# Transposes moved from TensorE to the DMA crossbar in a fused linear-attention and feed-forward kernel

## The chip, the cores and the metric

The kernel runs on one core of a Trainium2 chip. The metric is the device time of one execution in microseconds, median over several executions. An execution over 1.5% above the fastest of its kernel is called slow, and the others fast. A core has TensorE (PE, with its weight loads PEld), VectorE (DVE), ScalarE (ACT), GpSimd (POOL) and the sync engine (SP), and 16 DMA engines; the profile gives the packets of each DMA queue as a share of these 16 (it can sum to over 100%). Three queues issue DMAs here: sync's (q1), GpSimd's (q0) and, in one experiment, ScalarE's (q10). The granted clock is the share of its full speed that TensorE was given, as the trace records it.

## The reference, cut to what matters

```python
# q, k, v: (8 batches, 8 heads, 576 rows, 64), float32
phi(x)  = concat(relu(x) * cos_w, relu(x) * sin_w)      # 128 features per row
kv      = einsum('bhsf,bhsd->bhfd', phi(k), v);  z = sum of phi(k) over the rows
x       = (phi(q) @ kv) / (phi(q) @ z + 1e-6)           # -> (4608, 512)
out     = (((x @ w1) * (x @ w2)) @ w3) @ w_out          # -> (4608, 512)
```

The kernel transposes the left operand of two products, which has its rows on the partitions: the q features before `phi(q) @ kv`, and x before `x @ w1`. Each batch has five row chunks, four of 128 rows and one of 64.

## The kernel before: the parts that matter

`w3 @ w_out` is folded once. Then come the attention of batch 0 alone, step 0 of the feed-forward part (512 rows), the attention of batch 1 alone, and steps 1 to 8. Into step t, for t from 1 to 6, the attention of batch t + 1 is woven, and the loads of batch t + 3 are issued at its start (up to batch 7, so in steps 1 to 4).

```python
def load(b, eng):                       # k, v, q of one batch: 3 x (1 MB + 128 KB)
    ...
load(0, nc.gpsimd); ...w1, w2...; load(1, nc.gpsimd)     # cut; batches 2 to 7: nc.sync

def prep_k(b, c):                       # features of k; v gets a column of ones
    nc.vector.tensor_scalar(out=kp[...], in0=ks, ...)
    nc.scalar.activation(out=kp[...], in_=ks, func=ACTF.Relu, ...)
    nc.gpsimd.tensor_copy(out=va[:R, c, :, 0:D], in_=vs)

def q_tr(b, c):                         # transpose 8 heads of one chunk; cut: R, qp
    pst = ps_tr.tile([P, 8, 128], BF16, name="pst")
    for h in range(H):
        nc.tensor.transpose(pst[:, h, 0:R], qp[:R, c, h, :], identb[:R, :R])
    nc.vector.tensor_copy(out=att[b]["qpT"][:, :, ds(128 * c, R)], in_=pst[:, :, 0:R])

def num(b, c): ...                      # PE: numerator and denominator; DVE: den, xblk

def x_tr(b, c):                         # ... cut: which xT tile, which columns
    for kc in range(4):
        nc.tensor.transpose(pst[:, kc, 0:R], xf[:, ts(kc, 128)], identb[:R, :R])
    nc.scalar.copy(out=xT[t][:, :, ds(o, R)], in_=pst[:, 0:4, 0:R])

for t in range(NT):                     # cut: step 0, the bounds of t
    spread(prep_units(t + 2), 0, 22, slots); load(t + 3, nc.sync)
    spread(attention_units(t + 1), 0, 22, slots)   # 24 slots of a step
```

Of the kernel before, what the change touches and what calls it, by code (L numbers as in the profile page):

```python
# [11 lines left out]
BF16 = mybir.dt.bfloat16  # L12
# [4 lines left out]
P = 128  # L17
H, S, D = 8, 576, 64
F = 2 * D
NCH = 5  # L20
# [28 lines left out]
def kernel(  # L49
# [11 lines left out]
    nc = tc.nc  # L61
# [13 lines left out]
    ps_tr = ctx.enter_context(tc.tile_pool(name="ps_tr", bufs=2, space=bass.MemoryType.PSUM))  # L75
# [17 lines left out]
    identb = const.tile([P, P], BF16, name="identb")  # L93
# [11 lines left out]
    for i in range(2):  # L105
        va = const.tile([P, NCH, H, D + 1], BF16, name=f"va{i}")
# [4 lines left out]
    def load(b, eng):  # L111
        got = []
        for name, src in (("k", k), ("v", v), ("q", q)):
            t = ld.tile([P, H, 4, D], FP32, name=name + "s")
            eng.dma_start(out=t[:], in_=src[b, :, 0:512, :].rearrange("h (p j) d -> p h j d", j=4))
            t4 = ld.tile([64, H, D], FP32, name=name + "s4")
            eng.dma_start(out=t4[:], in_=src[b, :, 512:S, :].rearrange("h p d -> p h d"))
            got.append((t, t4))
        raw[b] = got
# [40 lines left out]
    def prep_k(b, c):  # L160

        R = ROWS[c]
        if c == 0:
            feat[b] = (
                phi.tile([P, NCH, H, F], BF16, name="kp"),
                phi.tile([P, NCH, H, F], BF16, name="qp"),
                va_bufs[b % 2],
            )
        kp, qp, va = feat[b]
        (k0, k4), (v0, v4), _ = raw[b]  # L170
        ks = k0[:, :, c, :] if c < 4 else k4[:]
        vs = v0[:, :, c, :] if c < 4 else v4[:]
        nc.vector.tensor_scalar(out=kp[:R, c, :, 0:D], in0=ks, scalar1=0.0,
                                scalar2=cosv[:R, c:c + 1], op0=ALU.max, op1=ALU.mult)
        nc.scalar.activation(out=kp[:R, c, :, D:F], in_=ks, func=ACTF.Relu,  # L175
                             scale=sinv[:R, c:c + 1], bias=0.0)
        nc.gpsimd.tensor_copy(out=va[:R, c, :, 0:D], in_=vs)  # L177

    def prep_q(b, c):

# [9 lines left out]
    att = {}  # L190

    def kv_chunk(b, c):
        R = ROWS[c]
        kp, qp, va = feat[b]
        if c == 0:
            att[b] = {
                "kv": ps_att.tile([P, 2, 512], FP32, name="pnum"),
                "qpT": phi.tile([P, H, S], BF16, name="qpT"),
                "x": {},
            }  # L200
        kvt = att[b]["kv"]
        for h in range(H):
            nc.tensor.matmul(kvt[:, h // 4, ds((h % 4) * 65, 65)], lhsT=kp[:R, c, h, :],  # L203
                             rhs=va[:R, c, h, :], start=(c == 0 and h % 4 == 0),
                             stop=(c == NCH - 1 and h % 4 == 3))
        if c == NCH - 1:
            kvs = sm.tile([P, H, D + 1], BF16, name="kvs")
            nc.scalar.copy(out=kvs[:, 0:4, :], in_=kvt[:, 0, 0:260])
            nc.vector.tensor_copy(out=kvs[:, 4:8, :], in_=kvt[:, 1, 0:260])
            att[b]["kvs"] = kvs  # L210

    def q_tr(b, c):
        R = ROWS[c]
        qp = feat[b][1]
        pst = ps_tr.tile([P, 8, 128], BF16, name="pst")
        for h in range(H):
            nc.tensor.transpose(pst[:, h, 0:R], qp[:R, c, h, :], identb[:R, :R])  # L217
        nc.vector.tensor_copy(out=att[b]["qpT"][:, :, ds(128 * c, R)], in_=pst[:, :, 0:R])  # L218

    def num(b, c):  # L220
        R = ROWS[c]
        qpT, kvs = att[b]["qpT"], att[b]["kvs"]
        nt = ps_att.tile([P, 2, 512], FP32, name="pnum")
        for h in range(H):
            nc.tensor.matmul(nt[:R, h // 4, ds((h % 4) * 65, 65)], lhsT=qpT[:, h, ds(128 * c, R)],  # L225
                             rhs=kvs[:, h, :], start=True, stop=True)
        n4 = nt[:R, :, 0:260].rearrange("p g (h e) -> p g h e", e=65)
        den = sm.tile([P, 2, 4], FP32, name="den")
        nc.vector.tensor_scalar_add(out=den[:R], in0=n4[:, :, :, 64], scalar1=1e-6)
        nc.vector.reciprocal(out=den[:R], in_=den[:R])  # L230
        xblk = sm.tile([P, 2, 4, D], BF16, name="xblk")
        nc.vector.tensor_tensor(out=xblk[:R], in0=n4[:, :, :, 0:D],  # L232
                                in1=den[:R].unsqueeze(3).to_broadcast([R, 2, 4, D]), op=ALU.mult)
        att[b]["x"][c] = xblk

    xT = {}

    def x_tr(b, c):
        R = ROWS[c]
        xblk = att[b]["x"].pop(c)  # L240
        xf = xblk[:R].rearrange("p g h d -> p (g h d)")
        if b % 2 == 0:
            slot = S * b + 128 * c
        else:
            slot = S * b + (0 if c == 4 else 64 + 128 * c)
        t, o = divmod(slot, 512)
        if t not in xT:
            xT[t] = xtp.tile([P, 4, 512], BF16, name="xT")
        pst = ps_tr.tile([P, 8, 128], BF16, name="pst")
        for kc in range(4):  # L250
            nc.tensor.transpose(pst[:, kc, 0:R], xf[:, ts(kc, 128)], identb[:R, :R])  # L251
        nc.scalar.copy(out=xT[t][:, :, ds(o, R)], in_=pst[:, 0:4, 0:R])  # L252

    def attention_units(b):

        order = [0, 1, 2, 3, 4] if b % 2 == 0 else [4, 0, 1, 2, 3]
        u = [(lambda c=c: kv_chunk(b, c)) for c in range(NCH)]
        u.insert(2, lambda: q_tr(b, order[0]))
        u.insert(5, lambda: q_tr(b, order[1]))
        for i in range(NCH + 1):  # L260
            if i < NCH:
                u.append(lambda c=order[i]: num(b, c))
            if i + 2 < NCH:
                u.append(lambda c=order[i + 2]: q_tr(b, c))
            if i >= 1:
                u.append(lambda c=order[i - 1]: x_tr(b, c))
        return u
# [42 lines left out]
    def prep_units(b):  # L310
        return ([(lambda c=c: prep_k(b, c)) for c in range(NCH)]
                + [(lambda c=c: prep_q(b, c)) for c in range(NCH)])
# [5 lines left out]
    for u in prep_units(0) + attention_units(0):  # L318
        u()

    def spread(units, first, last, slots):
        for i, u in enumerate(units):
            slots[min(last, first + int(i * (last + 1 - first) / len(units)))].append(u)

    for t in range(NT):
        slots = [[] for _ in range(24)]
        if t == 0:
            spread(prep_units(1), 15, 23, slots)
            slots[23] += prep_units(2)[0:4] + attention_units(1) + prep_units(2)[4:]
            load(2, nc.sync)  # L330
        else:
            if t + 2 < B:
                spread(prep_units(t + 2), 0, 22, slots)
                if t + 3 < B:
                    load(t + 3, nc.sync)
            if t + 1 < B:
                spread(attention_units(t + 1), 0, 22, slots)
        for g, _ in enumerate(ffn_groups(t)):
            for u in slots[g]:
                u()  # L340
        if t == 0:
            load(3, nc.sync)
# [30 lines left out]
```

## Time and profile before

| | before |
|---|---|
| median time (4 runs) | 306.85 us |
| span of the profiled run | 302.6 us |
| PE busy, share of the span | 89% |
| attention of batch 0 begins / step 0 / step 1 / step 2 begin | 43.5 / 57.7 / 93.5 / 120.9 us |
| a step with attention / without | 27.2 / 20.7 us |

The start of a step is the start of its first matmul with `w1b`. In the profile's lines "<-" inside a name pair reads "written from", and "idle before <- X" names what ended an engine's idle time. The lines that bound the kernel stand in the prediction.

### The profile page before, as it was taken

How to read it: one execution, taken by the hardware profiler on the slowest of the kernel's cores; microseconds unless marked ns; L12 is line 12 of the kernel's file. 1: busy time of each engine (PE TensorE's matmuls, PEld its weight loads, DVE VectorE, ACT ScalarE, POOL GpSimd, SP SyncE). 2: the span in 40 equal slices, each digit the busy share in tenths (PEclk: the TensorE clock that was granted, in tenths of full speed). 3: DMA queues.
4: the chain of work that ended last, by engine and by line, in shares of the span. 5: the costliest groups of instructions: out<-in, count | busy, mean ns of one | idle time of the engine just before them, and what ended most of it. 6: DMA issues, size and time to landing. Idle time of an engine off the chain costs nothing.

```text
span 302.6 us, 5330 instructions
## 1 busy us (share of the span) xinstructions
PE 268.1 (89%) x2112; PEld 145.0 (48%) x2112; DVE 160.6 (53%) x358; ACT 143.2 (47%) x249; POOL 45.8 (15%) x76
## 2 busy tenths in 40 slices
PE   1979027899877999999999999999999999999994
PEld 1444026444554554555555555555555555444441
DVE  7122607435677894488369637846872572330420
ACT  2033801335927756556656655575564225333322
POOL 8622650231004040012004000400000000000000
PEclk9999757599979999999999999999999999999999
DMA  7999999990499943791397269320013002103103
GB/s 99 194 277 276 212 257 289 261 230 9 143 287 269 268 112 96 211 267 54 131 289 178 68 192 264 88 109 32 0 44 97 2 0 105 37 0 118 23 15 124
DMA packets 41784, 43.33 MB, mean 143 GB/s; under 512 B 10848, under 2 KB 34912, under 8 KB 41760
## 3 DMA queue, kind: packets, MB, share of 16 engines
q1 hardware_dynamic: 33472, 30.68, 37.7%
q0 software_dynamic: 8288, 12.32, 19.4%
q8 instruction: 16, 0.26, 0.4%
q14 instruction: 8, 0.07, 0.1%
HBM read 38.80 MB, written 9.44 MB: 159 GB/s over the span
## 4 chain that ended last, share of the span: by engine, by line
PE 77%; DMA 11%; ACT 4%; DVE 3%; POOL 3%; issue 1%; POOLq 0%; ACTq 0%
PE ffnps L292 21%; PE ffnps L299 21%; PE ffnps L285 20%; DMA w2b<-in_moe_w_dram 5%; DMA ks<-in_k_dram 5%; PE pst L217 5%; PE pnum L225 4%; PE pnum L203 3%; PE pst L251 3%; DVE xblk L232 2%; ACT qp L187 1%; ACT kp L175 1%; POOL woutb L97 1%; POOL w3b L96 1%; DVE den L230 0%
## 5 line engine op out<-in xcount | busy, mean ns | idle before, releaser
L294 DVE TENSOR_TENSOR abT<-asb,ffnps 128x512 bf16<-128x512 bf16 x72 | 49.3, 685 | 71.8 <-PE ffnps L292 68.7
L288 ACT CAST asb<-ffnps 128x512 bf16<-128x512 f32 x72 | 42.1, 585 | 73.9 <-PE ffnps L285 67.6
L285 PE MATMUL ffnps<-xT,w1b 128*128 128x512 bf16 x288 | 74.7, 382 | 0.1
L292 PE MATMUL ffnps<-xT,w2b 128*128 128x512 bf16 x288 | 74.8, 382 | 0.0
L299 PE MATMUL ffnps<-w34b,abT 128*128 128x512 bf16 x288 | 69.6, 379 | 0.0
L177 POOL CAST va<-vs 128x512 bf16<-128x512 f32 (+1 forms) x40 | 24.3, 652 | 125.0 <-DMA vs<-in_v_dram 66.2
L285 PEld LDWEIGHTS <-w1b 128*128 128x128 bf16 x288 | 26.3, 98 | 25.9 <-issue 1.1
L299 PEld LDWEIGHTS <-abT 128*128 128x128 bf16 x288 | 26.2, 98 | 25.8
L292 PEld LDWEIGHTS <-w2b 128*128 128x128 bf16 x288 | 25.1, 98 | 24.3 <-issue 1.1
L252 ACT COPY xT<-pst 128x512 bf16<-128x512 bf16 (+1 forms) x40 | 21.8, 545 | 26.2 <-PE pst L251 25.2
L218 DVE COPY qpT<-pst 128x1024 bf16<-128x1024 bf16 (+1 forms) x40 | 25.2, 629 | 15.3 <-PE pst L217 15.3
L304 ACT COPY osb<-ffnps 128x512 f32<-128x512 f32 x36 | 21.1, 586 | 22.6 <-PE ffnps L299 16.1
L203 PE MATMUL pnum<-va,kp 128*128 128x65 bf16 (+1 forms) x320 | 17.2, 198 | 13.5 <-POOL va L177 13.5
L232 DVE TENSOR_TENSOR xblk<-pnum,den 128x512 bf16<-128x512 f32 (+1 forms) x40 | 27.6, 689 | 1.4
L187 ACT ACTIVATE qp<-qs,sinv 128x512 bf16<-128x512 f32 (+1 forms) x40 | 27.8, 720 | 0.2 <-DMA qs<-in_q_dram 0.2
L175 ACT ACTIVATE kp<-ks,sinv 128x512 bf16<-128x512 f32 (+1 forms) x40 | 27.8, 720 | 0.0
L203 PEld LDWEIGHTS <-kp 128*128 128x128 bf16 (+1 forms) x320 | 15.1, 101 | 22.8 <-issue 14.8
L217 PE MATMUL pst<-identb,qp 128*128 128x128 bf16 (+1 forms) x320 | 25.0, 225 | 0.9 <-ACT qp L187 0.8
L217 PEld LDWEIGHTS <-qp 128*128 128x128 bf16 (+1 forms) x320 | 20.7, 103 | 9.4 <-issue 1.3
L225 PE MATMUL pnum<-kvs,qpT 128*128 128x65 bf16 (+1 forms) x320 | 18.0, 200 | 5.4 <-DVE xblk L232 3.1
L225 PEld LDWEIGHTS <-qpT 128*128 128x128 bf16 (+1 forms) x320 | 15.4, 104 | 15.4 <-DVE xblk L232 4.9
L185 DVE TENSOR_SCALAR qp<-qs,cosv 128x512 bf16<-128x512 f32 (+1 forms) x40 | 21.0, 548 | 1.2 <-DMA qs<-in_q_dram 1.2
(46 smaller groups left out, 145.3 us busy)
## 6 DMA issues: line engine op xcount, KB each, us to landing
out_dram<-osb SPq DMA_DIRECT2D x32, 256.0 KB, 2.3
ks<-in_k_dram SPq DMA_DIRECT2D x6, 1024.0 KB, 8.0
vs<-in_v_dram SPq DMA_DIRECT2D x6, 1024.0 KB, 10.4
qs<-in_q_dram SPq DMA_DIRECT2D x6, 1024.0 KB, 10.8
ks<-in_k_dram POOLq DMA_DIRECT2D x2, 1024.0 KB, 17.6
vs<-in_v_dram POOLq DMA_DIRECT2D x2, 1024.0 KB, 21.2
qs<-in_q_dram POOLq DMA_DIRECT2D x2, 1024.0 KB, 23.0
w3b<-in_moe_w_dram POOLq DMA_DIRECT2D x3, 512.0 KB, 11.6
```

The source lines that it names most:

```text
L175: nc.scalar.activation(out=kp[:R, c, :, D:F], in_=ks, func=ACTF.Relu, scale=sinv[:R, c:c + 1], bias=0.0)
L187: nc.scalar.activation(out=qp[:R, c, :, D:F], in_=qs, func=ACTF.Relu, scale=sinv[:R, c:c + 1], bias=0.0)
L203: nc.tensor.matmul(kvt[:, h // 4, ds((h % 4) * 65, 65)], lhsT=kp[:R, c, h, :], rhs=va[:R, c, h, :], start=(c == 0 and h % 4 == 0), stop=(c ...
L217: nc.tensor.transpose(pst[:, h, 0:R], qp[:R, c, h, :], identb[:R, :R])
L218: nc.vector.tensor_copy(out=att[b]["qpT"][:, :, ds(128 * c, R)], in_=pst[:, :, 0:R])
L225: nc.tensor.matmul(nt[:R, h // 4, ds((h % 4) * 65, 65)], lhsT=qpT[:, h, ds(128 * c, R)], rhs=kvs[:, h, :], start=True, stop=True)
L232: nc.vector.tensor_tensor(out=xblk[:R], in0=n4[:, :, :, 0:D], in1=den[:R].unsqueeze(3).to_broadcast([R, 2, 4, D]), op=ALU.mult)
L285: nc.tensor.matmul(aT[:, :], lhsT=w1b[:, kc, ts(jc, 128)], rhs=x[:, kc, :], start=(kc == 0), stop=(kc == 3))
L288: nc.scalar.copy(out=asb[:], in_=aT[:, :])
L292: nc.tensor.matmul(bT[:, :], lhsT=w2b[:, kc, ts(jc, 128)], rhs=x[:, kc, :], start=(kc == 0), stop=(kc == 3))
L294: nc.vector.tensor_mul(out=abT[:, jc, :], in0=asb[:], in1=bT[:, :])
L299: nc.tensor.matmul(ops[:, :], lhsT=abT[:, jc, ts(ms, 128)], rhs=w34b[:, jc, :], start=(jc == 0), stop=(jc == 7))
```

## The change

The changed kernel lets a DMA transpose what it moves (`dma_start_transpose`, below a crossbar transpose); in the kernel before, TensorE's transposes go to tiles in PSUM and are copied out of them (an eviction, 629 ns on average for a q chunk). The intent: TensorE is the bound, so take 60 of a batch's 140 small matmuls off it, and with them the PSUM evictions on VectorE and ScalarE. The cast of v for the first two batches leaves GpSimd's queue, where it stands behind DMA issues. Each q transpose is issued right after a key-value chunk, long before its use.

```diff
-        nc.gpsimd.tensor_copy(out=va[:R, c, :, 0:D], in_=vs)
+        if b < 2:
+            nc.scalar.copy(out=va[:R, c, :, 0:D], in_=vs)
+        else:
+            nc.gpsimd.tensor_copy(out=va[:R, c, :, 0:D], in_=vs)
 ...q_tr
-        pst = ps_tr.tile([P, 8, 128], BF16, name="pst")
-        for h in range(H):
-            nc.tensor.transpose(pst[:, h, 0:R], qp[:R, c, h, :], identb[:R, :R])
-        nc.vector.tensor_copy(out=att[b]["qpT"][:, :, ds(128 * c, R)], in_=pst[:, :, 0:R])
+        nc.sync.dma_start_transpose(out=att[b]["qpT"][:, :, ds(128 * c, R)],
+                                    in_=qp[:R, c].rearrange("p h f -> p (h f)"))
 ...x_tr
-        (four PE transposes into PSUM and a ScalarE copy)
+        nc.sync.dma_start_transpose(out=xT[t][:, :, ds(o, R)], in_=xf)
 ...attention_units: kv_chunk(0), q_tr, kv_chunk(1), q_tr, ... then num and x_tr in turn
-                spread(attention_units(t + 1), 0, 22, slots)
+                spread(attention_units(t + 1), 0, 19, slots)
```

More of the change, by code (lines that the diff above doesn't have):

```diff
@@ L248, in x_tr @@
             xT[t] = xtp.tile([P, 4, 512], BF16, name="xT")
-        pst = ps_tr.tile([P, 8, 128], BF16, name="pst")
-        for kc in range(4):
-            nc.tensor.transpose(pst[:, kc, 0:R], xf[:, ts(kc, 128)], identb[:R, :R])
-        nc.scalar.copy(out=xT[t][:, :, ds(o, R)], in_=pst[:, 0:4, 0:R])
+        nc.sync.dma_start_transpose(out=xT[t][:, :, ds(o, R)], in_=xf)
     def attention_units(b):
         order = [0, 1, 2, 3, 4] if b % 2 == 0 else [4, 0, 1, 2, 3]
-        u = [(lambda c=c: kv_chunk(b, c)) for c in range(NCH)]
-        u.insert(2, lambda: q_tr(b, order[0]))
-        u.insert(5, lambda: q_tr(b, order[1]))
+        u = []
+        for c in range(NCH):
+            u.append(lambda c=c: kv_chunk(b, c))
+            u.append(lambda c=order[c]: q_tr(b, c))
         for i in range(NCH + 1):
@@ L262, in attention_units @@
                 u.append(lambda c=order[i]: num(b, c))
-            if i + 2 < NCH:
-                u.append(lambda c=order[i + 2]: q_tr(b, c))
             if i >= 1:
```

## The prediction

Terms of the sum: a q chunk was reckoned at 1.8 us of the queue (5 x 1.8 = 9 us for a batch), an output chunk at half of that, and 2.5 us to land. These were estimates; the trace before has no crossbar transpose to show them, only a 256 KB store that landed in 2.3 us. The sum came to 328 us of span, 332 us of time. A variant of rival (a) with faster transposes, near 299 us, is cut too, and so are the odds set on queueing in order. The lower clock after idle stretches, named at the end, is in the trace before: after 13.54 us of idle TensorE the granted clock was 0.50 from 43.5 to 47.2 us.

> **What bounds the kernel now.** I read the chain that ended last first, then busy time by stage, then the waits, then the sync engine's DMA queue in order of time. The chain's two lines:
>
> ```profile
> PE 77%; DMA 11%; ACT 4%; DVE 3%; POOL 3%; issue 1%; POOLq 0%; ACTq 0%
> PE ffnps L292 21%; PE ffnps L299 21%; PE ffnps L285 20%; DMA w2b<-in_moe_w_dram 5%; DMA ks<-in_k_dram 5%; PE pst L217 5%; PE pnum L225 4%; PE pnum L203 3%; PE pst L251 3%; DVE xblk L232 2%; ACT qp L187 1%; ACT kp L175 1%; POOL woutb L97 1%; POOL w3b L96 1%; DVE den L230 0%
> ```
>
> TensorE is the bound for 77%. The two transposes that leave, L217 (q) and L251 (attention output), are 5% + 3% = 8% of 302.6 us, or 24 us: the most that their removal can give on this path. The stages, from the order of TensorE's instructions: weights folded to 30 us; idle to 43.5; attention of batch 0 to 57.7; feed-forward step 0 to 79.7; attention of batch 1 to 93.5; then steps 1 to 6, each with the attention of the next batch woven in; steps 7 and 8 without. One woven step beside a bare one (columns: window, length, busy us and instruction count for PE, PEld, DVE, ACT, POOL, then clock, DMA share, GB/s):
>
> ```profile
> 175.50:202.60 27.10, 27.10 (x237) 14.88 (x236) 17.86 (x39) 16.02 (x28) 3.04 (x5) 1.00 0.65 169
> 257.00:277.70 20.70, 20.70 (x98) 9.41 (x96) 5.50 (x8) 7.03 (x12) 0.00 (x0) 1.00 0.13 47
> ```
>
> PE never rests in either; VectorE and ScalarE do. Attention costs a step 27.2 - 20.7 = 6.5 us. Early on one wait stands out:
>
> ```profile
> PE pnum L203 <- POOL va L177: 13.5, 1, 13.5
> ```
>
> GpSimd casts v of batch 0 only at 42.86 us, after the last DMA issue of its own queue, though v had landed near 30 to 31 us (the issue at 29.98 had waited for it). Last, the sync queue at the start of step 2, and what its loads take to land in the window 121 to 135 us:
>
> ```profile
> 121.80 0.33 SPq L306 DMA_DIRECT2D out_dram<-osb  x1
> 122.22 0.39 SPq L115 DMA_DIRECT2D ks<-in_k_dram  x1
> 122.70 0.67 SPq L117 DMA_DIRECT2D ks<-in_k_dram  x1
> 123.47 0.57 SPq L115 DMA_DIRECT2D vs<-in_v_dram  x1
> 124.13 4.37 SPq L117 DMA_DIRECT2D vs<-in_v_dram  x1
> 128.60 1.23 SPq L115 DMA_DIRECT2D qs<-in_q_dram  x1
> 129.92 2.71 SPq L117 DMA_DIRECT2D qs<-in_q_dram  x1
> ```
> ```profile
> ks<-in_k_dram SPq DMA_DIRECT2D x1, 1024.0 KB, 8.0
> qs<-in_q_dram SPq DMA_DIRECT2D x1, 1024.0 KB, 11.5
> qs<-in_q_dram SPq DMA_DIRECT2D x1, 128.0 KB, 10.6
> ```
>
> A batch's load holds the issuing queue from 122.2 to 132.6, 10.4 us, and its last bytes land at 129.92 + 10.6 = 140.5, 19.4 us after the step began at 121.1. Today nobody needs those bytes within the step, so the queue is free to be slow. This decides my prediction.
>
> [...] The trace has 233 ns as the mean of a transpose on TensorE, and eight of them pass in 0.44 us when pipelined (127.60 to 128.04), 55 ns each; a crossbar one isn't in the trace. [...] the 128 KB part of q, issued last, takes 10.6 us to land, whereas a 256 KB store on an empty queue takes 2.3 us. [...]
>
> **The change, part by part.**
>
> *TensorE.* Per batch, 40 q transposes (four chunks at 0.44 us, the short one about 0.25) = 2.0 us, and 20 of the output (four chunks at 0.22, one about 0.1) = 1.0 us. 3.0 us leaves each woven step, to 24.2 us; over six steps 18 us. This is on the path.
>
> *VectorE and ScalarE.* 40 qpT copies (25.2 us) and 40 xT copies (21.8 us) go. Both engines have slack in the steps; it is worth something only in the two bare attention stages.
>
> *Cast on ScalarE.* Five casts at about 0.6 us (like the 585 ns of L288), 3 us per batch. For batch 0, k features start at 30.6; kp and va together are 5 x (0.72 + 0.6) = 6.6 us, to 37.2, then q features to 40.8. The key-value matmuls can so end near 37.5 instead of 47.6. For batch 1 the casts sit in the last nine slots of step 0, where ScalarE has 9 x 0.72 + 5 x 0.6 + 4 x 0.59 = 11.9 us against 8 us of matmuls: some 4 us late into the second attention stage.
>
> *Crossbar transposes.* A q chunk is 128x1024 bf16, 256 KB; [...] a 256 KB store here lands in 2.3 us. [...] Stage 0: issued 38 to 47, last numerator about 48.5, its x block 1.3 us later, last output transpose landed at 52.5. **Step 0 starts at 52 to 53 instead of 57.7: -5 us.**
>
> *Attention of batch 1.* The built order puts its five q transposes behind the last store of step 0, which waits for ScalarE: 52.5 + 14.9 to the ninth slot from the end, + 11.9 of ScalarE = 79.3. So 79.5 + 9 of transposes + numerators and blocks, and the last output transpose is issued near 92, step 1 starts at 94.5 (before 93.5). The 5 us are lost again, and 1 more.
>
> *Loads against transposes.* In the built order of the sync queue, the loads of batches 3 and 4 now come after these transposes, where before they were issued from 81.25, and the q transposes of batch 2 come behind both. The two loads took from 81.25 to 102.05 + 9.0 = 111.05, 29.8 us. From 92.5 this makes 122, so the first q chunk of batch 2 lands near 123.5. TensorE needs it in slot 10 of step 1, about 10.5 us in, at 105. It waits 18 us. Behind slot 10 there are 13 groups of 4 matmuls at 0.86 us and five numerators at 0.27, 12.7 us: step 2 starts near **136 instead of 121.1: +15 us.** In steps 2, 3 and 4 the load of one batch stands ahead: last bytes at 19.4 us, first q chunk at 20, step 20 + 12.7 = 32.7 instead of 27.2: **+5.5 us each, +16.5.** Steps 5 and 6 have no loads: 24.2 each, **-6 us.** Steps 7 and 8 and the last store: unchanged.
>
> Sum of the span: 136 + 3 x 32.7 + 2 x 24.2 + (302.6 - 257.0) = 328 us; with the 3.7 us between the span and the median (306.27 - 302.6), 332 us.
>
> **The rivals.**
> (a) *The transposes hide.* If they do not queue behind the loads' bytes, only behind their issue, the first q chunk of a step lands at 1.1 + 10.4 + 2 = 13.5 us, the step is 26.2, and step 2 starts at 92 + 26 + 12.7 = 131: 131 + 78.6 + 48.4 + 45.6 = 304, a time near 307. [...] For it: the DMA share is 0.65 in the loaded steps and 0.1 in those after. Against: the landing times above.
> (b) *All of the 18 us, and the early wait, are won*: 27 us, a time near 280. It needs the loads to leave the path; the built order speaks against it.
> (c) *The crossbar is slow*, 3 us a q chunk and half that an output chunk: 4.5 x 4.5 = 20 us of the queue per batch. The bare stages grow by 6 and 5 us, step 1 by more, each loaded step by some 5: a time near 350 to 360. The profile has no transposing DMA, so nothing excludes it.
>
> **Range and chances.** The reckoned sum is 332; (a) draws towards 307 and below, (c) towards 355. [...] take 322 as my middle, since in-order queueing is seen only in landing times of loads. Range 296 to 350. Slower by over 2% (above 312.4) 0.73, within 2% 0.15, faster (below 300.1) 0.12.
>
> **What would show each step right or wrong.** Right: TensorE idle in front of the numerator matmul in steps 1 to 4, released by the DMA of qpT, about 18 us in step 1 and 9 in each of steps 2 to 4; loads of batch 3 issued after 88 us; steps 5 and 6 at 24 us; step 0 starting at 52 to 53; key-value matmuls of batch 0 starting about 32. Wrong: qpT landing within 3 us of its issue while loads are in flight, idle TensorE released by xT instead (the output transposes as the new wait), or an issue on the sync queue taking well over 2 us per q chunk, which would make the queue itself the bound. A lower granted clock after idle stretches would lengthen the matmuls beyond this sum.

## The result, and the profile after

The changed kernel takes **354.0 us** (352.74 to 354.95, 4 runs) against 306.85 us: 15.2% slower, ratio 1.152 with a 95% interval of 1.144 to 1.160. Ratios here are the mean time of one kernel's fast runs over that of the other's fast runs in the same rounds, so they are not quite the ratio of the medians. The direction was forecast; the size was not, and the time lies outside the range of 296 to 350.

The page of the changed kernel, the chain that ended last by engine and line:

```profile
PE 58%; DMA 17%; DVE 7%; SPq 3%; issue 2%; ACT 2%; DVEq 0%; ACTq 0%
PE ffnps L296 18%; PE ffnps L282 17%; PE ffnps L289 17%; DMA qpT<-qp 15%; PE pnum L226 4%; DVE xblk L233 3%; PE pnum L206 2%; SPq L117 2%; DMA xT<-xblk 1%; DVE abT L291 1%; DVE den L231 1%; ACT kp L175 1%; SPq L115 1%; DMA out_dram<-osb 1%; DVE den L230 1%
```

The transposes on TensorE are gone from the chain (they were 8%); the DMA that writes qpT has come in with 15%. The group of the numerator matmuls tells the same as a wait: 60.3 us of idle TensorE ended by qpT.

```profile
L226 PE MATMUL pnum<-kvs,qpT 128*128 128x65 bf16 (+1 forms) x320 | 20.5, 216 | 78.9 <-DMA qpT<-qp 60.3
```

Where these waits lie is told by the starts of the steps (us, from the order of TensorE's instructions; "reckoned" is the sum in the prediction):

| start of step | 0 | 1 | 2 | 3 | 4 | 5 | 6 | 7 | end |
|---|---|---|---|---|---|---|---|---|---|
| before | 57.7 | 93.5 | 120.9 | 148.1 | 175.3 | 202.5 | 229.7 | 256.9 | 302.6 |
| reckoned | 52.5 | 94.5 | 136 | 168.7 | 201.4 | 234.1 | 258.3 | 282.5 | 328 |
| after | 71.2 | 110.9 | 155.2 | 188.6 | 222.4 | 256.7 | 281.6 | 305.9 | 351.7 |

A loaded step and one without loads (window, length, busy us and count of PE, PEld, DVE, ACT, POOL, then granted clock, DMA share, GB/s):

```profile
188.58:222.42 33.84, 26.39 (x173) 12.65 (x176) 14.89 (x34) 13.49 (x23) 2.85 (x5) 0.90 0.85 190
282.00:306.00 24.00, 23.47 (x172) 11.59 (x175) 10.95 (x24) 7.11 (x13) 0.00 (x0) 1.00 0.63 117
```

Without loads the change does what it was meant to do: 24.0 us in this window, 24.3 from start to start, for about 27.2. With loads a step takes 33.8. The sync queue in the first of these two windows shows why (start, length, instruction):

```profile
189.82 0.45 SPq L115 DMA_DIRECT2D ks<-in_k_dram  x1
...
196.44 2.84 SPq L117 DMA_DIRECT2D qs<-in_q_dram  x1
199.37 10.07 SPq L218 DMA_TRANSPOSE qpT<-qp  x5
```

The q transposes are issued only after the six DMAs of the load, 10.8 us into the step, and then queue behind their bytes: the last part of the load, issued at 196.44, and the first q transpose, issued at 199.37, took to land (us, windows 197 to 199 and 200 to 203)

```profile
qs<-in_q_dram SPq DMA_DIRECT2D x1, 128.0 KB, 9.3
qpT<-qp SPq DMA_TRANSPOSE x1, 7.2
```

So the load ends at 205.7 and the first q chunk is there at 206.6, 18.0 us into the step. Of the 7.2 us some 4 are the queueing (an estimate: a q chunk without a load before it lands in 2.7 to 3.4). TensorE's first numerator of that batch is held 6.85 us; in the step before, by the same path, it looks so:

```profile
165.35 1.03 PE L282 MATMUL ffnps<-xT,w1b 128*128 128x512 bf16 x4
173.34 0.65 PE L226 MATMUL pnum<-kvs,qpT 128*64 128x65 bf16 x8 [6.96 <-DMA qpT<-qp]
173.92 1.89 PE L289 MATMUL ffnps<-xT,w2b 128*128 128x512 bf16 x4
```

Four matmuls took 1.03 us before the wait and 1.89 after it: the granted clock is 0.50 from 173.3 to 176 us, after the gap, and 1.00 again from 178 on; the mean of the step is 0.90.

The waits were in the prediction. What was not is the first gap, ahead of step 0. TensorE and the sync queue there:

```profile
37.45 0.60 PE L206 MATMUL pnum<-va,kp 64*128 64x65 bf16 x8 [0.53 <-ACT va L178]
61.16 0.62 PE L226 MATMUL pnum<-kvs,qpT 128*128 128x65 bf16 x8 [23.12 <-DMA qpT<-qp]
```
```profile
38.05 24.85 SPq L218 DMA_TRANSPOSE qpT<-qp  x5
62.98 8.81 SPq L250 DMA_TRANSPOSE xT<-xblk  x5
...
97.63 6.72 SPq L218 DMA_TRANSPOSE qpT<-qp  x5
```

The cast on ScalarE did its work: the key-value matmuls were through at 38 us. But five q transposes held the queue for 24.85 us, where those of batch 1, with no other queue at work (window 98 to 104 us), took 6.72. No load is ahead of them on their own queue. What is beside them is GpSimd's queue (q0), still loading w2 and batch 1. The DMA queues in the window 46 to 48 us (packets, MB, share of 16 engines; q1 is sync's):

```profile
q0 software_dynamic: 118, 0.44, 89.8%
q1 hardware_dynamic: 118, 0.03, 12.6%
```

As many packets on one queue as on the other, but 3.7 KB each on one and 256 bytes on the other: the transposes get a fourteenth of the load's bytes. The counts look as if the two queues took turns, a packet at a time (118 and 118); this is the author's reading of them, and the turns themselves are not in the trace. The kernel before had shown equal counts, in the window 40 to 42 us, where both sides were loads:

```profile
q0 software_dynamic: 255, 0.24, 70.6%
q1 hardware_dynamic: 255, 0.26, 46.4%
```

There the packets were of about 1 KB on both sides, so nobody starved. But in the window 46 to 48 us the same kernel has the starving too, without any crossbar transpose: GpSimd's queue has come to the large packets of batch 1, sync's to the 256-byte rows of its own load.

```profile
q0 software_dynamic: 177, 0.63, 96.0%
q1 hardware_dynamic: 164, 0.04, 11.8%
```

The 128 KB of k that sync loads in such packets landed 20.8 us after its issue at 33.77, the 1 MB of k just before it, in packets of 1 KB, 13.4 us after its own. So the profile before held the warning.

### The profile page after: what moved, and what is told of

It is laid out like the page before. It is cut to its first block, busy times and chain, and to the rows that moved or that the text cites. A ratio compares the mean times of both kernels' runs of the same rounds, so it can differ in the third digit from the quotient of the medians.

```text
span 351.7 us, 4494 instructions
## 1 busy us (share of the span) xinstructions
PE 249.2 (71%) x1604; PEld 122.1 (35%) x1632; DVE 136.8 (39%) x318; ACT 127.6 (36%) x219; POOL 38.5 (11%) x66
## 4 chain that ended last, share of the span: by engine, by line
PE 58%; DMA 17%; DVE 7%; SPq 3%; issue 2%; ACT 2%; DVEq 0%; ACTq 0%
PE ffnps L296 18%; PE ffnps L282 17%; PE ffnps L289 17%; DMA qpT<-qp 15%; PE pnum L226 4%; DVE xblk L233 3%; PE pnum L206 2%; SPq L117 2%; DMA xT<-xblk 1%; DVE abT L291 1%; DVE den L231 1%; ACT kp L175 1%; SPq L115 1%; DMA out_dram<-osb 1%; DVE den L230 1%
## 5 line engine op out<-in xcount | busy, mean ns | idle before, releaser
L282 PE MATMUL ffnps<-xT,w1b 128*128 128x512 bf16 x280 | 78.2, 400 | 4.7 <-DMA xT<-xblk 3.6
L289 PE MATMUL ffnps<-xT,w2b 128*128 128x512 bf16 x277 | 78.3, 403 | 0.4
L226 PE MATMUL pnum<-kvs,qpT 128*128 128x65 bf16 (+1 forms) x320 | 20.5, 216 | 78.9 <-DMA qpT<-qp 60.3
L296 PE MATMUL ffnps<-w34b,abT 128*128 128x512 bf16 x281 | 63.9, 379 | 0.3
L282 PEld LDWEIGHTS <-w1b 128*128 128x128 bf16 x288 | 28.5, 102 | 37.5 <-issue 9.1
L180 POOL CAST va<-vs 128x512 bf16<-128x512 f32 (+1 forms) x30 | 17.1, 614 | 181.7 <-DMA vs<-in_v_dram 181.7
L230 DVE TENSOR_SCALAR den<-pnum 128x8 f32<-128x8 f32 (+1 forms) x40 | 6.5, 163 | 70.1 <-PE pnum L226 70.1
L173 DVE TENSOR_SCALAR kp<-ks,cosv 128x512 bf16<-128x512 f32 (+1 forms) x40 | 18.2, 477 | 4.8 <-DMA ks<-in_k_dram 4.8
L133 PE MATMUL ffnps<-woutb,w3T 128*128 128x512 bf16 x62 | 18.2, 422 | 2.2 <-DVE w3T L145 1.2
L188 DVE TENSOR_SCALAR qp<-qs,cosv 128x512 bf16<-128x512 f32 (+1 forms) x40 | 18.1, 486 | 0.4 <-DMA qs<-in_q_dram 0.4
L143 ACT COPY w3T<-pst 128x512 bf16<-128x512 bf16 x8 | 4.7, 586 | 21.5 <-PE pst L140 21.5
## 6 DMA issues: line engine op xcount, KB each, us to landing
w3b<-in_moe_w_dram POOLq DMA_DIRECT2D x3, 512.0 KB, 12.7
```

What stands on the lines that cost most here:

```text
L133: nc.tensor.matmul(acc[jp][:, :], lhsT=w3T[:, ts(jp, 128)], rhs=woutb[:, lc, :], start=(lc == 0), stop=(lc == 7))
L226: nc.tensor.matmul(nt[:R, h // 4, ds((h % 4) * 65, 65)], lhsT=qpT[:, h, ds(128 * c, R)], rhs=kvs[:, h, :], start=True, stop=True)
L282: nc.tensor.matmul(aT[:, :], lhsT=w1b[:, kc, ts(jc, 128)], rhs=x[:, kc, :], start=(kc == 0), stop=(kc == 3))
L289: nc.tensor.matmul(bT[:, :], lhsT=w2b[:, kc, ts(jc, 128)], rhs=x[:, kc, :], start=(kc == 0), stop=(kc == 3))
L296: nc.tensor.matmul(ops[:, :], lhsT=abT[:, jc, ts(ms, 128)], rhs=w34b[:, jc, :], start=(jc == 0), stop=(jc == 7))
```

## The experiments

Two causes are to be told apart from rivals: loads ahead on the same queue (steps 1 to 4), and large packets on another queue (ahead of step 0). Eleven kernels ran. All gave right results but one. A time without an interval is one run with a profile. The kernel before ran beside them with medians of 304.8 to 306.7 us.

**1. The cast alone.** The kernel before with the first hunk of the diff only.

> The kernel before with nothing but the cast of v on ScalarE for batches 0 and 1; all transposes stay on TensorE. My theory: the 13.5 us wait of the first key-value matmul for GpSimd falls to under 4 us, step 0 starts at 50 to 52 us instead of 57.7, of which 2 to 4 us are given back in the second attention stage because ScalarE has 3 us more to do in the last third of step 0. Time 299 to 303 us. Rival: step 0 is held by w1 and w2 landing near 42 to 48 us or by the q features on ScalarE, then step 0 starts at 55 or later and the time stays above 304 us.

Measured: 302.69 us (302.45 to 302.9), ratio 0.990 (0.986 to 0.994). Step 0 starts at 50.3 us, 7.4 sooner. Step 1 starts at 89.1, 4.3 sooner: TensorE waits for q features on ScalarE, which has the casts of batch 1 to do as well (window 70 to 96 us):

```profile
72.63 0.68 PE L206 MATMUL pnum<-va,kp 128*128 128x65 bf16 x16
76.36 0.40 PE L220 MATMUL pst<-identb,qp 64*128 64x64 bf16 x8 [3.04 <-ACT qp L190]
```

Step 2 starts only 2.0 us sooner (118.9): step 1 begins slowly, with 1.90 us for four matmuls at 91.3 us and 1.03 from 95.3 on. So this part of the change is good for 1%, and the whole loss, and more, comes with the crossbar transposes and the new order of units.

**2. The load beside the first transposes, taken away.** In the changed kernel:

```diff
-    load(1, nc.gpsimd)
 ...
     for u in prep_units(0) + attention_units(0):
         u()
+    load(1, nc.sync)
```

> The changed kernel with the load of batch 1 moved from GpSimd's queue to the sync queue, behind the transposes of batch 0. In the changed kernel the first numerator waits 23.1 us for a q transpose that shares the DMA engines with that load, and between 46 and 52 us the two queues finished 387 and 386 packets, of 3.7 KB and 256 bytes. Theory (engines take packets of the two queues in turn, so 256-byte packets starve beside large ones): with that load gone the wait falls from 23 us to under 8, step 0 starts at 54 to 58 us instead of 71, and the time falls by about 14 us to 338 to 343. Rival (a crossbar transpose is slow at its first use, or waits for its features): the wait stays above 18 us and step 0 starts at 68 or later.

Measured: 344.63 us (343.54 to 346.15), ratio 1.127 (1.122 to 1.132). The wait fell to 8.16 us and step 0 starts at 55.7, both as the theory has it; the line to set beside that of 61.16 above:

```profile
45.75 0.62 PE L225 MATMUL pnum<-kvs,qpT 128*128 128x65 bf16 x8 [8.16 <-DMA qpT<-qp]
```

The rival is out: its wait of over 18 us did not come. Of the 15.4 us won at step 0, 10.9 are left at the start of step 1 (100.0), because the load of batch 2 now comes behind that of batch 1 and the second attention stage waits 10.14 us through VectorE for the key-value copy on ScalarE, while the stores of step 0 were issued only at 78.74, behind those loads; hence the small miss of the forecast time.

**3. No loads in the steps.** In the changed kernel `load(b)` for b of 3 and up only sets `raw[b] = raw[b - 2]` (wrong result).

> The changed kernel without the loads of batches 3 to 7, whose attention reads the tiles of batches 1 and 2 again (wrong result on purpose). Theory (the transposes of steps 1 to 4 wait behind the loads): steps 1 to 4, now 44.3, 33.4, 33.8 and 34.2 us, all fall to the 24.5 to 25 us of steps 5 and 6, and the span to about 304 us; stage 0 stays at 71 us. Rival (the crossbar's own pace, or the order of numerators and output transposes, sets these steps): they stay above 29 us and the span above 325.

Measured: 309.66 us, span 307.8. Steps 2 to 4 take 24.8, 24.9 and 24.8 us, step 1 takes 27.7 and step 0 starts at 70.4. Step 3, to compare with the row of 33.84 above:

```profile
163.12:188.01 24.89, 23.88 (x173) 11.71 (x176) 14.78 (x34) 13.49 (x23) 3.07 (x5) 1.00 0.52 113
```

With the loads gone, steps 1 to 4 are 43.6 us shorter, of the span's 43.9, and only step 1 is not as short as forecast: it begins slowly (1.90 us for four matmuls at 112.7 us, as at the clock of 0.50 above). It keeps a small loss against the kernel before (27.7 and 27.5 us); steps 2 to 4 are faster than there. The crossbar's own pace does not set a step.

**4. Transposes in the steps without loads only.** From the kernel before with the cast, `q_tr` and `x_tr` use the crossbar `if b in (6, 7)`, in the changed kernel's order, else TensorE.

> The kernel before with the cast on ScalarE and with crossbar transposes for batches 6 and 7 alone, whose steps have no loads. Theory: steps 5 and 6 take 24.5 us instead of 27.2, so 5.4 us less than the cast alone; about 295 us, the first version to beat both. Rival: a q transpose wait appears here too, or the gain is eaten by the last steps: no more than 2 us below the cast alone.

Measured: 297.28 us (295.51 to 298.08), ratio 0.971 (0.967 to 0.976), 5.4 us below the cast alone. A step with TensorE's transposes and the next with the crossbar's, in this one kernel:

```profile
173.75:200.93 27.18, 26.97 (x233) 14.88 (x236) 17.44 (x39) 16.00 (x28) 3.10 (x5) 1.00 0.64 169
200.93:225.83 24.90, 23.90 (x174) 11.73 (x176) 14.39 (x33) 13.49 (x23) 0.00 (x0) 1.00 0.59 110
```

**5. The loads on GpSimd's queue.** The changed kernel with `load(t + 3, nc.gpsimd)` and `load(3, nc.gpsimd)`.

> The changed kernel with the loads of batches 3 to 7 issued from GpSimd's queue, so that no load stands ahead of a transpose on the sync queue in steps 1 to 4. Theory (the engines alternate packets of the two queues, 256 bytes against some 3.7 KB): the q transposes still starve until the load is through, some 14 to 16 us into the step, so numerators still wait 4 us or more and steps 2 to 4 take 28 to 31 us, against 33.4 to 34.2. Rival (only the order on the sync queue counts, and the engines share bytes fairly): the first q chunk lands in 3 to 5 us, no numerator waits, steps 2 to 4 fall to 24.5 to 26 us.

Measured: 356.04 us. The loads now run ahead into the second attention stage, and there five q transposes, 6.72 us in the changed kernel, take 21:

```profile
98.17 20.99 SPq L218 DMA_TRANSPOSE qpT<-qp  x5
```

The queues in the window 108 to 110 us:

```profile
q0 software_dynamic: 157, 0.61, 87.3%
q1 hardware_dynamic: 163, 0.04, 11.8%
```

Again nearly equal packets (157 and 163) and a fifteenth of the bytes. But steps 2, 3 and 4 took 32.3, 26.6 and 24.8 us, not the 28 to 31 forecast: neither theory has that spread. GpSimd issues most of a load in the step before (batch 7's k and v from 216 us, step 4 starts at 234), so step 4 holds only its q part. I drew from it that loads do little harm if they come at another time, which run 7 tested.

**6. One cast, and the output transposes too.** Run 4 with the cast on ScalarE for batch 0 only; then the same with `x_tr` on the crossbar `if b in (2, ..., 7)` and the units of those batches spread over slots 0 to 20 instead of 22.

> Crossbar transposes for batches 6 and 7 alone, as before, but the cast on ScalarE for batch 0 only. With two batches cast there, a q transpose of batch 1 waits 3.0 us for ScalarE in the second attention stage. Theory: that wait goes, step 1 starts 3 us sooner and the time falls from 297 to about 294 us. Rival: GpSimd's cast of batch 1 now comes late because its load lands late, or the ScalarE copies of the key-value product set the stage anyway: no change within 1 us.

> The same, with the attention output of batches 2 to 5 transposed by the crossbar too, their q features still on TensorE. The output transposes come in the second half of a step, when the load's bytes have nearly landed, and are needed only by the next step. Theory: each of steps 1 to 4 loses its 1.0 us of output transposes and waits for nothing, so 4 us less than without, about 290 us. Rival: they queue behind the load and the next step waits for xT, by over 2 us per step: slower than without, 297 us or more.

Measured: 295.59 us (293.44 to 296.75), ratio 0.968 (0.962 to 0.975); and **291.27 us (290.3 to 293.45), ratio 0.954 (0.948 to 0.960), the best**. The first starts step 1 at 86.8 instead of 90.6 us, but its time gained less than the 3 us forecast, and the intervals of the two ratios overlap. The second is 4.3 us below the first, 4 forecast (by the medians; its profiled run is the slowest of its four, and the two profiled spans, 293.0 and 291.7, differ by 1.3). Its steps 2 to 4 took 26.8 us instead of 27.2, a gain of 0.4 each where 1.0 was forecast, and step 1 28.0 instead of 29.8. In such a step TensorE's busy time falls by the 1.1 us meant (27.19 to 26.11), but 0.69 us of idling comes in front of the first numerator, which now waits for VectorE's copy of the key-value product. The output transposes landed in 2.5 us (median), and no feed-forward matmul waited for xT: they come late in a step and are needed only in the next.

**7. More q transposes, with loads on GpSimd's queue.** The best version with `load(t + 3, nc.gpsimd)`, and q by the crossbar for batches 4 to 7, 3 to 7, or 6 and 7 (the control).

> The best so far (291.3 us: cast of batch 0 on ScalarE, output of batches 2 to 7 and q of 6 and 7 by the crossbar) with the loads of batches 4 to 7 on GpSimd's queue and q of batches 4 and 5 by the crossbar as well. With all loads there, the changed kernel's steps 3 and 4 took 26.6 and 24.8 us although they load. Theory: what a q transpose can't bear is bytes of a load in front of it or beside it in the first half of a step, not loads as such; GpSimd issues most of a load in the half step before. Steps 3 and 4, now 26.8 us, fall to 24.8 to 26; time 286 to 290 us. Rival: the q load, which is issued at the turn of the steps, still collides with the transposes: numerators wait over 2 us a step and the time is 292 us or more.

> The same with q of batch 3 by the crossbar too, whose step 2 follows the step with two loads in it. Theory: step 2 gains as steps 3 and 4 do, 1 to 2 us below the version with batches 4 to 7. Rival: loads are still crowded there, as in the changed kernel with all loads on GpSimd, where step 2 took 32 us: 2 us or more slower than the version with batches 4 to 7.

> The control: the loads of batches 4 to 7 on GpSimd's queue, q by the crossbar for batches 6 and 7 alone, output for 2 to 7. Theory: nothing waits for those loads within a step, so their queue alone changes nothing: within 1.5 us of 291.3. Rival: GpSimd's own casts come late behind its DMA issues, and key-value matmuls wait for them: 293 us or more.

Measured: 302.82 us (301.67 to 308.97), ratio 0.989 (0.984 to 0.994); 302.67 us (301.1 to 308.59), ratio 0.988 (0.982 to 0.993); the control 294.85 us (294.65 to 295.6), ratio 0.965 (0.960 to 0.970). One run of each of the first two was slow; it is in the medians and not in the ratios. My theory fell. With q of batches 4 and 5 by the crossbar, step 4 takes 24.8 us, but step 3 takes 36.8. GpSimd's queue, TensorE and the sync queue in it:

```profile
156.02 0.89 POOL L115 DMA_DIRECT2D vs<-in_v_dram  x1
```
```profile
172.88 0.62 PE L232 MATMUL pnum<-kvs,qpT 128*64 128x65 bf16 x8 [8.85 <-DVE xblk L239]
```
```profile
156.33 10.21 SPq L257 DMA_TRANSPOSE xT<-xblk  x3
```

The load of batch 7 meets the output transposes; three of them hold the queue 10.2 us, their x blocks stay in use (three buffers), VectorE waits 10.5 us for them in two waits of the run, and TensorE 8.85 us for VectorE. Packets taken in turn do not explain all of it: between 158 and 162 us 50 packets of the load and 1,235 of sync's queue ran. In these runs a load delayed transposes from either queue (a q chunk landed 7.2 us after its issue behind a load on sync's queue, 17.2 beside one on GpSimd's in run 5), and the bytes only moved from one step to another. The control is some 1% slower than with the loads on sync, not the "nothing" forecast; the two ran in different rounds. Its trace has step 1 at 31.1 us instead of 28.0: loads are crowded into it, and TensorE waits 1.33 us for the key-value copy, 1.04 for an x block and, at the start of step 2, 1.26 for xT.

**8. The load of batch 1 in smaller packets.** In the changed kernel `load(1, nc.scalar)` after `prep_units(0)`.

> The changed kernel with the load of batch 1 issued from ScalarE's queue, behind the features of batch 0, so that it runs beside the q transposes again, but in packets of 1 KB and 256 bytes (rows as the sync queue's loads have them) and not of the 3.7 KB that GpSimd's queue makes. A packet count is the measure, not the total time: ScalarE is held up by its own issues, which delays the copies of the key-value product to 50 us or later. Theory (one packet of each queue in turn): packet counts of the two queues stay equal in each 2 us while both have work, but the transposes now get a quarter of the load's bytes or more instead of a fourteenth; the first q chunk lands within 12 us of its issue instead of 22.8. Rival (any load beside a transpose starves it alike): the first q chunk still takes 18 us or more.

Measured: 351.44 us, which says little, as foretold: ScalarE's copy of the key-value product came only at 55.22 us, behind its DMA issues (the last at 54.57). The three queues in the window 42 to 44 us (q10 is ScalarE's):

```profile
q0 software_dynamic: 218, 0.22, 65.4%
q10 hardware_dynamic: 218, 0.22, 31.3%
q1 hardware_dynamic: 218, 0.06, 21.1%
```

Three queues, 218 packets each, bytes as their packet sizes. The transposes now get a quarter of each neighbour's bytes, and the first q chunk landed 12.4 us after its issue instead of 23.1, beside the same load (its q part was issued only at 53.39 us, but ScalarE's queue had packets in every 2 us from 38 us up to the landing) and with two neighbours instead of one. That is just over the 12 forecast and far from the rival's 18. So in these windows the share left to a transpose went with the size of the neighbour's packets (a fourteenth of its bytes beside 3.7 KB, a quarter beside 1 KB), not with the mere presence of a load.

## Why the prediction was wrong

**The step that failed** is this one: "Stage 0: issued 38 to 47, last numerator about 48.5, its x block 1.3 us later, last output transpose landed at 52.5." It gave the transposes of batch 0 an empty set of DMA engines. Step 0 started at 71.2, 18.7 us later than reckoned, of the 23.7 us between the reckoned span of 328 and the measured 351.7. Runs 2 and 8 showed the cause: the load of batch 1 on GpSimd's queue, whose packets are 14 times as large, beside transposes that move no more packets than it: from 42 to 54 us 882 packets of the load and 861 of sync's queue ran, where the first q chunk alone has 1,024 of 256 bytes. And the page of the kernel before shows the DMA engines full (0.9 or more busy) from 7.6 to 68 us, and its traces 128 KB in small packets taking over 20 us to land beside that load.

The other terms, in order:

- *Cast on ScalarE.* Key-value matmuls from 32.9 to 38.0 us, forecast near 32 to 37.5: right, and run 1 puts step 0 at 50.3 with TensorE's transposes.
- *Pace of a transpose.* 1.8 us a q chunk was assumed, 0.9 an output chunk, 2.5 us to land. Without a load beside them they took 6.72 / 5 = 1.34 us (128x1024 in bf16) and 1.2 us (128x512) on the queue, so between these two, halving the chunk saves almost nothing, and landed in 2.7 us at best for q and 2.4 (median) for the output. Close; rival (c), a slow crossbar, is out. The time fell into its range for another reason. By an estimate from the DMA shares, the transposes cost the DMA engines more per byte than loads: those of one batch (1.77 MB) took 0.55 x 24.6 = 13.5 us of the engines in a step without loads (257.4 to 282), of which some 2.9 us (0.14 x 20.6, the bare step from 306) are stores: about 10.6 us, or 167 GB/s. The load of a batch (3.54 MB) took 0.65 x 27.1 - 0.10 x 27.2 = 14.9 us in the kernel before, about 238 GB/s.
- *Attention of batch 1.* From step 0 to step 1 42 us were reckoned, 39.8 measured.
- *Loads in front of transposes.* Step 1 41.5 reckoned, 44.3 measured; steps 2 to 4 32.7 each, measured 33.4, 33.8 and 34.2; the waits in front of the numerators 18 and 9, measured 15.7 and 6.9 to 7.6. Right in mechanism (run 3) and within 3 us a step, but by two errors that offset each other. The first q chunk of step 3 landed 18.0 us into the step, not 20. What follows the first numerator took 15.8 us, not 12.7 (the terms given, 13 x 0.86 + 5 x 0.27, make 12.5): in step 5, where nothing waits, it is 14.0 us, and the rest goes with the low clock after the wait (0.50 in step 2), which the prediction named but did not count.
- *Steps without loads.* 24.2 reckoned, 24.9 and 24.4 measured, and confirmed by run 4.

The sum: 18.7 - 2.2 + 2.8 + 3.3 + 0.9 + 0.2 = 23.7 us, for stage 0, batch 1, step 1, steps 2 to 4, steps 5 and 6, and the tail. A second mistake was in the weighing: the middle of 322 was pulled below the reckoned 332 by rival (a), transposes that hide, which no loaded step showed. The 3.7 us added for the time outside the span were 2.3 (354.0 - 351.7).

What stays open: between 56 and 60 us in the changed kernel the transposes went slowly, 319 and 212 packets per 2 us, when GpSimd's queue had only 27 and 18 packets left. Nor did any packet of the transposes run in the first 2 us after their issue at 38.05 (window 38 to 40; one packet from 40 to 42), and run 8 has none from their issue at 37.11 to 40 us either. Alternation alone does not explain these stretches, and no run tells what does. An obvious remedy was not tried: issuing each step's load behind its q transposes on the sync queue, as run 2 did for batch 1 alone.

## What to carry to other kernels

A transpose by DMA is not free because TensorE no longer does it: in these traces it stands in line behind the bytes of its own queue (first chunk 18.0 us into a step), and beside GpSimd's load it moved as many packets in 2 us (118 and 118), but of 256 bytes against 3.7 KB. So put it where no load is in flight, or where its result is wanted much later (here: q of the two batches without loads, and the attention output; 4.6% faster, with the cast of batch 0 on ScalarE, of which the cast for two batches alone gives 1%), and leave the transposes that are wanted soon on TensorE. Before moving work onto a DMA, list for its first use what every queue has in flight at that moment, and the packet size of each.
